# A late product with v and the next pair's transposes, each moved by one step in an attention and Fourier-mix kernel

## The chip, the cores and the metric

The kernel runs on one core of one Trainium2 chip. The metric is the device time of one execution in microseconds (us). All times in the text are in us unless a unit stands beside them.

## The reference

Attention with a threshold on 8 batches of 8 heads (576 rows of 64), and after it a Fourier mix and a two-layer network on rows of 512. Everything is float32.

```python
def _attn_ref(q, k, v, tau):
    scores = scale * np.matmul(q, k.transpose(0, 1, 3, 2))
    thresh = np.max(scores, axis=-1, keepdims=True) - tau
    scores = np.where(scores >= thresh, scores, -1000000000.0)
    scores = scores - np.max(scores, axis=-1, keepdims=True)
    attn = np.exp(scores)
    attn = attn / (np.sum(attn, axis=-1, keepdims=True) + 1e-09)
    return np.matmul(attn, v).astype(np.float32)
...
    X = np.fft.fft(x, axis=1)
    X = np.fft.fft(X, axis=2)
    u = x + np.real(X).astype(np.float32)
    un = (u - mu) / np.sqrt(var + 1e-06)
    ch = np.maximum(un @ w_ch1, 0.0) @ w_ch2
    return (u + ch).astype(np.float32)
```

Here x is the attention's output with the heads side by side, and mu and var are the mean and variance of each row of u.

## The kernel before, in words

**Pairs and steps.** The attention works on pairs of heads: four pairs a batch, 32 in all, numbered n from 0. A pair has five steps, t = 0 to 4. In the first four, 128 query rows of both heads are worked on; the fifth has the last 64 rows of both heads together. A step is written (n, t), and i = 5n + t. Every instruction of every engine stands in the order in which the program issues it (the schedule is made by hand), so what the loop issues first on an engine runs first there.

**The main loop** (L1774) runs over i from 40 on, that is from pair 8. In step i it issues, in this order:

1. `scores(i)`: q times k on TensorE into two score buffers (L439; in the fifth step L445, which reads a small copy of q made by `prep_ends`). The two buffers are those of the step before, so a score matmul waits until VectorE's last reading of them (L539).
2. For some steps the matmuls of a product with v (`values_in_parts`, L734). Each pair has two such products: part 0 for the query rows of t = 0 and 1, part 1 for those of t = 4, 2 and 3.
3. `softmax_first(i)`: two row maxima on VectorE (L518), then exponentials and a threshold on ScalarE (L524, L528).
4. The product's copies from PSUM to x on ScalarE (L740, L741 for part 1, L743 for part 0).
5. `fetch` for earlier steps (below), then `fill(True)`: a portion of the network's background work.
6. `softmax_second(i)`: compare, multiply and sum on VectorE (L539), and the reciprocal of the sum (L543, L546).
7. `decide(i - 1)`, `blocks(i - 1)`, some folding of x, `weights_in_parts(i - 1)`, `fill()`, `softmax_third(i)` (two ScalarE scalings, L552), `keep_blocks(i - 1)`, preparations for the next pair, and another `fill()`.

**Two ways for the weights.** The softmax's result e has to be turned round before it can be multiplied with v. Either TensorE transposes it and ScalarE copies it into the tile et_all (L637 to L668). Or, from pair 12 on and where `decide` says so, it goes through DRAM: VectorE transposes it in squares of 32 (`blocks`, L601) into one staging tile, ScalarE's queue writes that tile to DRAM as e_blocks (`keep_blocks`, L606), and the sync queue (SP) brings it back into et_all in four transfers (`fetch`, L615). There is one staging tile, so an L601 waits until the write before it has landed. `decide` picks the DRAM way for the first four steps of a pair when the background work is in the first of its two phases (`phase[0] == 1`), and for t = 2 after a DRAM step. In the trace these are (13,1) to (13,3), (14,0) to (14,3) and (15,0), and the same every four pairs up to (31,0): 40 steps.

**et_all** is in three groups of four blocks. t = 0 fills the first group, t = 1 and t = 2 the second in turn, t = 3 the third, t = 4 half of the first (blocks 2 and 3). Part 0 reads the first two groups; part 1 reads from block 2 on. So whatever writes blocks 2 and 3 for the next pair must come after part 1.

**When the products run, before.** Part 0 of pair n runs at the top of (n, 3), or at the top of (n+1, 0) if (n, 1) went through DRAM. Part 1 of pair n runs in (n+1, 1): at the top, or, if (n, 3) went through DRAM, after `fill(True)` with its copies right behind it (`late_values`, L1790 and L1805). There are ten such pairs: 13, 14, 17, 18, 21, 22, 25, 26, 29 and 30.

**The next pair.** q and k are loaded at the ends of (n, 0) and (n, 1), q is scaled on ScalarE in (n, 2), and `prep_pair(n + 1)` transposes them on VectorE at the end of (n, 3) (L410, L411, L413). `scores` of (n+1, 0) read the result. For pairs with their heads reversed (the first two of a batch) `v_of` makes a reversed copy of v on GpSimd (L584, L590); this happens in `weights_in_parts(i)` for t = 0, that is in step (n, 1).

**Background.** `fill` runs the network for groups of 512 rows as a budget allows: in phase 1 matmuls L1298 with additions on VectorE (L1235) and relus on ScalarE (L1240), in phase 2 matmuls L1447 with left-hand forms on VectorE and GpSimd (L1279). Their right-hand blocks are brought in through SP (L1171), in the same queue as the fetches, the loads of q, k and v, and the stores.

Of the kernel before, what the change touches and what calls it, by code (L numbers as in the profile page):

```python
# [47 lines left out]
def kernel(  # L48
# [13 lines left out]
    B, H, S, D = q.shape  # L62
# [3 lines left out]
    NPAIR = H // 2  # L66
    NT = 5
# [320 lines left out]
    heads = {}  # L388
# [171 lines left out]
    by_dma = {}  # L560
    phase = [0]

    def in_blocks(n):

        return n >= 3 * NPAIR
# [5 lines left out]
    def decide(i):  # L571

        n, t = divmod(i, NT)
        by_dma[i] = i < B * NPAIR * NT and in_blocks(n) and t < 4 and (
            phase[0] == 1 or t == 2 and by_dma[i - 1]
        )

    def v_of(n):

        src = heads[n][2]  # L580
        if PAIRS[n % NPAIR] % 2 == 0:
            return src
        vt = sb.tile([128, 10, D], FP32, tag="vr", bufs=1, name="v_rev")
        nc.gpsimd.tensor_copy(vt[:, :, 0:1], src[:, :, 0:1])  # L584
        last = src[:, :, D - 1 : D]
        down = bass.AP(
            tensor=last.tensor, offset=last.offset,
            ap=[list(last.ap[0]), list(last.ap[1]), [-1, D - 1]],
        )
        nc.gpsimd.tensor_copy(vt[:, :, 1:D], down)  # L590
        return vt
# [3 lines left out]
    def blocks(i):  # L595

        if not by_dma[i]:
            return
        e = steps.pop(i)[0]
        out_ = et_room.rearrange("p (b c q) -> p c b q", b=4, c=NC9)  # L600
        nc.vector.transpose(out_, e[:, 0 : 2 * S])  # L601
# [24 lines left out]
    def weights_in_parts(i):  # L626

        n, t = divmod(i, NT)
        if in_blocks(n) and t == 0:
            heads[n] = (*heads[n][0:2], v_of(n), None, None)  # L630
        if by_dma.get(i):
            return
        e, rec = steps.pop(i)
        if in_blocks(n) and t < 4:
            to = by_block[:, first_block(t) : first_block(t) + 4]
            pe = ps.tile([128, 4, 128], FP32, tag="mm", bufs=4, name="pe")
            nc.tensor.transpose(pe[:, 0, :], e[:, 512:640], ident[:, :])  # L637
            nc.scalar.copy(to[:, :, 4, :], pe[:, 0, :].rearrange("p (a q) -> p a q", q=32))  # L638
            for j in range(2):
                pw = ps.tile([128, 4, 128], FP32, tag="mm", bufs=4, name="pw")  # L640
                if j == 1:
                    yield
                for c in range(4):
                    c0 = (S + D) * j + 128 * c
                    nc.tensor.transpose(pw[:, c, :], e[:, c0 : c0 + 128], ident[:, :])  # L645
                nc.scalar.copy(
                    to[:, :, 5 * j : 5 * j + 4, :],
                    pw[:, :, :].rearrange("p c (a q) -> p a c q", q=32),
                )
            return  # L650
        if in_blocks(n):
            pe = ps.tile([128, 4, 128], FP32, tag="mm", bufs=4, name="pe")
            nc.tensor.transpose(pe[:, 0, :], e[:, 512:640], ident[:, :])
            for j in range(2):
                hp = slice(64 * j, 64 * j + 64)
                nc.scalar.copy(
                    by_block[hp, 2:4, 4, :],
                    pe[hp, 0, hp].rearrange("p (a q) -> p a q", q=32),
                )
            pw = ps.tile([128, 4, 128], FP32, tag="mm", bufs=4, name="pw")  # L660
            for c in range(4):
                nc.tensor.transpose(pw[:, c, :], e[:, 128 * c : 128 * c + 128], ident[:, :])
            for j in range(2):
                for a in range(2):
                    nc.scalar.copy(
                        by_block[:, 2 + a, 5 * j : 5 * j + 4, :],
                        pw[:, :, 64 * j + 32 * a : 64 * j + 32 * a + 32],
                    )  # L668
            return
        if t in (0, 2):  # L670

            e_t, ends = early_e_t, early_ends
            vt = v_of(n) if t == 0 else heads[n][2]
            heads[n] = (*heads[n][0:2], vt, e_t, ends)
        e_t, ends = heads[n][3:5]
        q0 = 128 * (t - (0 if t < 2 else 2))
        pe = ps.tile([128, 4, 128], FP32, tag="mm", bufs=4, name="pe")
        nc.tensor.transpose(pe[:, 0, :], e[:, 512:640], ident[:, :])  # L680
        kept = 1
        if rec is not None:
            nc.tensor.transpose(pe[:, 1, :], rec, ident[:, :])
            kept = 2
        if t < 4:
            nc.scalar.copy(ends[:, 0:kept, q0 : q0 + 128], pe[:, 0:kept, :])
        else:
            for j in range(2):
                hp = slice(64 * j, 64 * j + 64)
                nc.scalar.copy(ends[hp, 0:kept, q0 : q0 + 64], pe[hp, 0:kept, hp])  # L690
        qs = slice(q0, q0 + (128 if t < 4 else 64))
        for j in range(2 if t < 4 else 1):
            pw = ps.tile([128, 4, 128], FP32, tag="mm", bufs=4, name="pw")
            if j == 1:
                yield
            for c in range(4):
                c0 = (S + D) * j + 128 * c
                nc.tensor.transpose(pw[:, c, :], e[:, c0 : c0 + 128], ident[:, :])  # L698
            if t < 4:
                nc.scalar.copy(e_t[:, 4 * j : 4 * j + 4, qs], pw[:, :, :])  # L700
            else:
                nc.scalar.copy(
                    e_t[:, :, qs].rearrange("p (j c) q -> p j c q", j=2),
                    pw[:, :, :].rearrange("p c (j q) -> p j c q", j=2),
                )
# [846 lines left out]
    total = B * per_batch  # L1552
# [117 lines left out]
    def fold_more():  # L1670
        if folds and next(folds[0], True):
            folds.pop(0)
# [101 lines left out]
    for i in range(2 * per_batch, total + 3):  # L1774


        n, t = divmod(i, NT)
        values = iter(())
        if i < total:
            scores(i)  # L1780
        late_values = None
        if t == 3 and i < total and not by_dma.get(i - 2):
            values = values_in_parts(n, 0)
        elif t == 0 and by_dma.get(i - 4):
            values = values_in_parts(n - 1, 0)
        elif t == 1 and n > 0:
            while folds:
                fold_more()
            values = values_in_parts(n - 1, 1)
            if by_dma.get(i - 3):  # L1790
                values, late_values = iter(()), values
        next(values, None)
        if i < total:
            softmax_first(i)
        next(values, None)
        if t == 0 and by_dma.get(i - 4):
            fetch(i - 3)
        if t != 4 or not by_dma.get(i - 3):
            fetch(i - 2)
        if i % per_batch == 2:  # L1800
            for _ in last_fold:
                pass
            start_batch(i // per_batch - 1)
        fill(True)
        for _ in late_values or ():  # L1805
            pass
        if i < total:
            softmax_second(i)
        while held:
            held.pop(0)()  # L1810
        decide(i - 1)
        blocks(i - 1)
        while swaps:
            swaps.pop(0)()
        if mixes:
            mix(1)
        if t == 1:
            if n % NPAIR:
                folds.append(fold_rows(n - 1))
            else:  # L1820
                last_fold = fold_rows(n - 1)
                next(last_fold)
        weights = weights_in_parts(i - 1) if i <= total else iter(())
        next(weights, None)
        if t > 2:
            fold_more()
        fill()
        if i % per_batch == 1:
            next(last_fold)
        next(weights, None)  # L1830
        if i < total:
            softmax_third(i)
        keep_blocks(i - 1)
        if i < total:
            if t == 1:
                prep_ends(n)
            if t == 2 and n + 1 < B * NPAIR:
                scale_q(n + 1)
            if t == 3 and n + 1 < B * NPAIR:
                prep_pair(n + 1)  # L1840
        if wanted:
            wanted.pop().factors()
        if i % per_batch == 1:
            next(last_fold)
        fill()
        if t == 2 and n + 1 < B * NPAIR:
            load_v(n + 1)
        if t < 2 and n + 1 < B * NPAIR and len(loaded.get(n + 1, ())) == t:
            load_raw(n + 1, slice(t, t + 1))
# [50 lines left out]
```

## Time and profile before

| | |
|---|---|
| median of three runs | 1653.06 us (1650.37 to 1654.93) |
| the profiled execution | 1660.9 us |
| its span, first to last instruction | 1659.1 us |
| mean granted TensorE clock | 0.972 |
| transfers, mean over the span | 173 GB/s |

In the page's groups each line has the program's line, the engine, the operation with its output and inputs and their shapes, the count, the busy time and mean length, and after the bar the idle time of the engine just before these instructions with what ended most of it. In a timeline each line is a run of like instructions: start, length, engine, line, operation, and in square brackets the idle time ahead with its releaser. TensorE records two passes for each of these matmuls, so a count such as x20 stands for ten.

Steps differ in length with what they hold. In the stretch from pair 26 to pair 27 they run (start and length):

| step | start | length |
|---|---|---|
| (26,1) | 1138.4 | 9.4 |
| (26,2) | 1147.8 | 6.5 |
| (26,3) | 1154.3 | 6.3 |
| (26,4) | 1160.6 | 8.4 |
| (27,0) | 1169.0 | 11.0 |
| (27,1) | 1180.0 | 16.8 |
| (27,2) | 1196.8 | 7.3 |
| (27,3) | 1204.1 | 14.3 |

### The profile page before, as it was taken

The page shows a single profiled execution, that of the slowest core. Times are in us where ns is not written, and L with a number is a line of the kernel's source. Part 1 is how long each engine was busy: PE and PEld are TensorE (multiplying, and loading weights), DVE is VectorE, ACT ScalarE, POOL GpSimd, SP SyncE. Part 2 cuts the span into 40 slices and gives each one's busy share as a digit, 9 for nine tenths or more (in the row PEclk, how much of TensorE's full clock was granted, in tenths as well). Part 3 has the DMA queues.
Part 4 walks back from the last instruction along what each step waited for, and adds up shares of the span by engine and source line. Part 5 has one row for each costly group of instructions (what it writes and reads, how often), then busy time and mean ns, then how long its engine had stood idle before and what let it go on. Part 6 is the DMA issues. An engine that isn't in the chain of part 4 may idle for free.

```text
span 1659.1 us, 27069 instructions
## 1 busy us (share of the span) xinstructions
PE 1529.6 (92%) x9410; PEld 1166.8 (70%) x9410; DVE 1138.9 (69%) x2137; ACT 907.0 (55%) x1913; POOL 817.8 (49%) x1002
## 2 busy tenths in 40 slices
PE   8998889999999988999799988999799988999997
PEld 4555445556788766877588766787587767889987
DVE  7998786747678675767567765857567765645537
ACT  5765665545656565656466564666456655233231
POOL 6785663044454633544154724454154625546646
PEclk9999999999999998999999998999999999999999
DMA  6423222556855687648774777657775776657765
GB/s 160 120 55 111 73 73 50 191 174 169 256 168 143 177 225 208 186 110 230 199 201 135 196 220 208 175 131 219 208 195 129 213 210 189 205 152 218 245 183 194
DMA packets 296254, 286.26 MB, mean 173 GB/s; under 512 B 202643, under 2 KB 241045, under 8 KB 295222
## 3 DMA queue, kind: packets, MB, share of 16 engines
q1 hardware_dynamic: 287846, 260.64, 57.5%
q10 hardware_dynamic: 8272, 23.89, 4.0%
q8 instruction: 76, 1.25, 0.3%
q14 instruction: 60, 0.49, 0.1%
HBM read 231.10 MB, written 53.22 MB: 171 GB/s over the span
## 4 chain that ended last, share of the span: by engine, by line
PE 55%; DVE 19%; DMA 11%; ACT 7%; issue 4%; POOL 2%; SPq 1%; ACTq 0%; DVEq 0%; POOLq 0%
PE po L1447 14%; PE ph L1298 13%; PE pv L734 8%; PE sc L439 5%; PE po L1025 4%; DMA et_all<-e_blocks 3%; DMA w<-f 3%; DMA e_blocks<-w 2%; PE ph L1001 2%; ACT e L524 2%; DVE e L479 2%; PE pw L645 2%; DVE e L539 2%; PE pw L698 2%; PE py L874 2%
## 5 line engine op out<-in xcount | busy, mean ns | idle before, releaser
L524 ACT ACTIVATE e<-sc,neg 128x576 f32<-128x576 f32 x216 | 158.6, 734 | 132.3 <-DVE neg L518 131.5
L1447 PE MATMUL po<-w,w_all 128*128 128x128 f32 x1792 | 229.3, 278 | 1.2 <-ACT et_all L638 0.7
L518 DVE TENSOR_REDUCE neg<-sc 128x1 f32<-128x576 f32 x216 | 153.7, 748 | 110.0 <-PE sc L439 101.3
L1447 PEld LDWEIGHTS po<-w,w_all 128*128 128x128 f32 x1792 | 214.2, 193 | 11.5 <-issue 5.3
L1244 POOL TENSOR_TENSOR w<-hs 128x512 f32<-128x512 f32 x32 | 42.3, 1326 | 334.7 <-ACT hs L1240 334.7
L539 DVE SCALAR_TENSOR_TENSOR e<-sc,thr,e 128x576 f32<-128x576 f32 x216 | 168.3, 812 | 54.7 <-ACT thr L528 54.7
L1298 PE MATMUL ph<-u_t,w 128*128 128x256 f32 x768 | 183.0, 383 | 0.0
L439 PE MATMUL sc<-kT,qT 64*128 64x288 f32 x1024 | 171.2, 433 | 9.5 <-DVE e L479 9.0
L1298 PE MATMUL ph<-w_all,w 128*128 128x256 f32 x672 | 159.4, 384 | 12.0 <-DVE hs L1235 11.6
L552 ACT ACTIVATE e<-e,den 128x576 f32<-128x576 f32 x216 | 156.8, 769 | 24.2 <-DVE den L546 23.7
L1298 PEld LDWEIGHTS ph<-u_t,w 128*128 128x128 f32 x768 | 142.4, 190 | 29.8 <-issue 8.2
L1298 PEld LDWEIGHTS ph<-w_all,w 128*128 128x128 f32 x672 | 125.1, 190 | 42.8 <-issue 13.6
L734 PE MATMUL pv<-et_all,v_in 128*64 128x256 f32 (+1 forms) x640 | 106.5, 488 | 41.5 <-DMA et_all<-e_blocks 17.4
L1235 DVE TENSOR_TENSOR hs<-ph,hs 128x512 f32<-128x512 f32 x64 | 60.5, 945 | 119.5 <-PE ph L1298 114.3
L439 PEld LDWEIGHTS sc<-kT,qT 64*128 64x128 f32 x1024 | 94.1, 187 | 65.0 <-issue 36.3
L1347 POOL TENSOR_TENSOR w_all<-w_all 128x128 f32<-128x128 f32 (+2 forms) x160 | 121.8, 779 | 32.7 <-DVE w_all L1465 22.4
L1240 ACT ACTIVATE hs<-hs 128x512 f32<-128x512 f32 x64 | 54.0, 843 | 135.0 <-DVE hs L1235 135.0
L1447 PE MATMUL po<-w,hs 128*128 128x128 f32 x960 | 125.7, 278 | 0.0
L1447 PEld LDWEIGHTS po<-w,hs 128*128 128x128 f32 x960 | 116.6, 193 | 8.9 <-issue 7.5
L734 PEld LDWEIGHTS pv<-et_all,v_in 128*64 128x64 f32 x640 | 55.8, 163 | 88.5 <-issue 52.1
L734 PE MATMUL pv<-et_all,v_rev 128*64 128x256 f32 (+1 forms) x640 | 84.7, 411 | 7.3 <-DMA out_dram<-u 4.7
L916 POOL TENSOR_TENSOR u_t<-x,tmp 128x289 f32<-128x289 f32 (+1 forms) x45 | 34.7, 770 | 105.3 <-DVE tmp L911 105.3
(235 smaller groups left out, 3216.9 us busy)
## 6 DMA issues: line engine op xcount, KB each, us to landing
w<-f SPq DMA_DIRECT2D x304, 512.0 KB, 4.5
e_blocks<-w ACTq DMA_DIRECT2D x40, 576.0 KB, 3.7
et_all<-e_blocks SPq DMA_DIRECT2D x160, 144.0 KB, 4.3
hs<-in_moe_w_ch_dram SPq DMA_DIRECT2D x23, 512.0 KB, 4.6
q_in<-in_q_dram SPq DMA_DIRECT2D x128, 72.0 KB, 4.6
out_dram<-u SPq DMA_DIRECT2D x36, 256.0 KB, 4.3
k_in<-in_k_dram SPq DMA_DIRECT2D x124, 72.0 KB, 4.2
v_in<-in_v_dram SPq DMA_DIRECT2D x64, 128.0 KB, 4.7
```

Of the source, the lines that this page charges most:

```text
L439: nc.tensor.matmul(sc[j][:, c, 0:HALF], qT[hp, 128 * t : 128 * t + 128], kT[hp, k0 + HALF * c : k0 + HALF * (c + 1)], start=True, stop=True,)
L518: nc.vector.tensor_reduce(out=neg[:, j : j + 1], in_=sc[j][:, :, 0:HALF], axis=AXIS_XY, op=ALU.max, negate=True,)
L524: nc.scalar.activation(out=ej, in_=sc[j][:, :, 0:HALF], func=ACT.Exp, bias=neg[:, j : j + 1], scale=1.0)
L539: nc.vector.scalar_tensor_tensor(out=ej, in0=sc[j][:, :, 0:HALF], scalar=thr[:, j : j + 1], in1=ej, op0=ALU.is_ge, op1=ALU.mult, accum_out ...
L552: nc.scalar.activation(out=e[:, S * j : S * (j + 1)], in_=e[:, S * j : S * (j + 1)], func=ACT.Copy, scale=den[:, j : j + 1],)
L734: nc.tensor.matmul(pv[64 * j : 64 * j + 64, 0:m], vt[:, 2 * c + j, :], right, start=(c == 0), stop=(c == 4), skip_group_check=True,)
L1025: nc.tensor.matmul(po[:, :], hs[:, BT * j + 128 * t : BT * j + 128 * (t + 1)], w2[j], start=(j == 0), stop=(j == NJ - 1),)
L1235: nc.vector.tensor_tensor(out=to, in0=bank, in1=to if other is None else other, op=ALU.add)
L1240: nc.scalar.activation(out=to, in_=to, func=ACT.Relu)
L1298: nc.tensor.matmul(bank[:, 256 * q : 256 * q + 256].rearrange("p (two n) -> p two n", two=2), left[:, 256 * c + 128 * q : 256 * c + 128 * ...
L1347: return lambda: eng.tensor_tensor(out=to, in0=to, in1=other, op=ALU.add)
L1447: nc.tensor.matmul(to, lefts[m][j][:, s], right_[:, 128 * s : 128 * (s + 1)], start=fresh and s == 0, stop=s == 3, skip_group_check=True,)
```

## The change

Part 1 of a pair whose (n, 3) went through DRAM is issued one step later, at the top of (n+1, 2), with its copies where those of other products stand. For that, `decide` also sends a step t = 0 through DRAM when the step two before it went that way (`by_dma[i - 2]` is (n-1, 3)); v's reversed copy is made in (n, 2) after `fill(True)`, behind the product, and no longer in (n, 1); and the folding of that pair's x is put in the list in (n+1, 2). Apart from that, `prep_pair(n + 1)` is issued in (n, 4), right behind `blocks(i - 1)`, and no longer at the end of (n, 3). This second edit holds for all pairs of the main loop.

```diff
         by_dma[i] = i < B * NPAIR * NT and in_blocks(n) and t < 4 and (
-            phase[0] == 1 or t == 2 and by_dma[i - 1]
+            phase[0] == 1 or t == 2 and by_dma[i - 1] or t == 0 and by_dma[i - 2]
         )
...
     def weights_in_parts(i):
 
         n, t = divmod(i, NT)
-        if in_blocks(n) and t == 0:
-            heads[n] = (*heads[n][0:2], v_of(n), None, None)
         if by_dma.get(i):
             return
...
-        late_values = None
         if t == 3 and i < total and not by_dma.get(i - 2):
             values = values_in_parts(n, 0)
         elif t == 0 and by_dma.get(i - 4):
...
         elif t == 1 and n > 0:
             while folds:
                 fold_more()
+            if not by_dma.get(i - 3):
+                values = values_in_parts(n - 1, 1)
+        elif t == 2 and by_dma.get(i - 4):
             values = values_in_parts(n - 1, 1)
-            if by_dma.get(i - 3):
-                values, late_values = iter(()), values
         next(values, None)
...
         fill(True)
-        for _ in late_values or ():
-            pass
+        if t == 2 and i < total and in_blocks(n):
+            heads[n] = (*heads[n][0:2], v_of(n), None, None)
         if i < total:
             softmax_second(i)
...
         decide(i - 1)
         blocks(i - 1)
+        if t == 4 and n + 1 < B * NPAIR:
+            prep_pair(n + 1)
         while swaps:
             swaps.pop(0)()
         if mixes:
             mix(1)
-        if t == 1:
+        if t == (2 if by_dma.get(NT * n - 2) else 1):
             if n % NPAIR:
                 folds.append(fold_rows(n - 1))
             else:
+                assert t == 1
                 last_fold = fold_rows(n - 1)
                 next(last_fold)
...
                 prep_ends(n)
             if t == 2 and n + 1 < B * NPAIR:
                 scale_q(n + 1)
-            if t == 3 and n + 1 < B * NPAIR:
-                prep_pair(n + 1)
```

## The prediction

> **What bounds the kernel now.** I read the page first, then the waits of the tile pv, then TensorE's and VectorE's timelines of one cycle of four pairs, then the table by stretch. A step is named (pair, t). Its start is its first score matmul (L439, L445).
>
> ```profile
> PE 1529.6 (92%) x9410; PEld 1166.8 (70%) x9410; DVE 1138.9 (69%) x2137; ACT 907.0 (55%) x1913; POOL 817.8 (49%) x1002
> L734 PE MATMUL pv<-et_all,v_in 128*64 128x256 f32 (+1 forms) x640 | 106.5, 488 | 41.5 <-DMA et_all<-e_blocks 17.4
> ```
>
> TensorE is busy 92%, so a gain has to come from its idle time, or from time at a low clock. The products with v (L734) have 41.5 us of idle ahead of them, mostly put down to a transfer. TensorE from (26,4) to (27,3):
>
> ```profile
> 1161.77 1.89 PE L1298 MATMUL ph<-u_t,w 128*128 128x256 f32 x8
> 1165.35 1.99 PE L1298 MATMUL ph<-w_all,w 128*128 128x256 f32 x8 [1.70 <-DVE hs L1235]
> ...
> 1169.01 1.24 PE L439 MATMUL sc<-kT,qT 64*128 64x288 f32 x8
> 1171.56 2.38 PE L734 MATMUL pv<-et_all,v_in 128*64 128x256 f32 x20 [1.31 <-DMA et_all<-e_blocks]
> ...
> 1181.14 1.99 PE L1298 MATMUL ph<-w_all,w 128*128 128x256 f32 x8
> 1188.60 5.47 PE L734 MATMUL pv<-et_all,v_in 128*64 128x320 f32 x20 [5.47 <-DMA q_in<-in_q_dram]
> 1194.00 1.99 PE L1298 MATMUL ph<-w_all,w 128*128 128x256 f32 x8
> ...
> 1207.77 3.90 PE L734 MATMUL pv<-et_all,v_in 128*64 128x256 f32 x20 [2.46 <-ACT e L524]
> ```
>
> The columns are start, length, what ran, and in brackets the idle ahead. At 1188.60 stands the late second product of pair 26 in (27,1): 5.47 us idle, then 20 records in 5.47 us where 2.7 would do. A last transfer into et_all was issued at 1183.73; q_in, named as releaser, is not among its operands, so I take it as that landing. The first product of pair 27 waits too (1207.77). At 1165.35 TensorE waits for VectorE, whose timeline says why:
>
> ```profile
> 1161.64 1.36 DVE L601 STREAM_TRANSPOSE w<-e 128x1152 f32<-128x1152 f32 x1
> 1162.92 0.73 DVE L410 STREAM_TRANSPOSE kT<-k_in 128x576 f32<-128x576 f32 x1
> 1163.67 0.24 DVE L411 STREAM_TRANSPOSE kT<-k_in 64x64 f32<-64x64 f32 x1
> 1163.94 0.78 DVE L413 STREAM_TRANSPOSE qT<-q_in 128x576 f32<-128x576 f32 x1
> 1164.65 0.65 DVE L1235 TENSOR_TENSOR hs<-ph,hs 128x512 f32<-128x512 f32 x1
> ...
> 1168.64 1.38 DVE L601 STREAM_TRANSPOSE w<-e 128x1152 f32<-128x1152 f32 x1 [0.47 <-DMA e_blocks<-w]
> ```
>
> The add that TensorE wants (L1235) stands behind the next pair's transposes. The five late products of this kind by stretch (us, busy times, then clock, DMA share, GB/s), first and last:
>
> ```profile
> 1180.00:1196.80 16.80, 11.33 (x53) 7.01 (x52) 5.96 (x11) 3.45 (x8) 0.00 (x0) 0.80 0.70 156
> 1367.50:1382.20 14.70, 10.47 (x55) 6.77 (x54) 6.03 (x11) 3.52 (x8) 0.00 (x0) 0.88 0.54 138
> ```
>
> A step of 16.8 us with 6.0 us of VectorE and 3.5 of ScalarE in it, at 0.80 of the clock: idle, and half clock after it.
>
> **What the Trainium skill says.** "TensorE: Matmul & The Clock Gate", Part 1: after an idle window of about 3.4 us the clock is halved until a busy one has passed. The stretch 1188.5 to 1193.6 has a clock of 0.50, so it agrees; but 2.46 us of idle also brought 0.55 (1207.7 to 1211.2), and 1.31 us none. The same page, Architectural detail: VectorE and ScalarE take instructions strictly in order; the L1235 above shows it. "DMA: Bandwidth & Descriptors", Issuing engines are not separate DMA queues: transfers of all queues share the same 16 engines. In (26,4) the DMA share is 1.03 at 306 GB/s, and ScalarE's e_blocks write issued at 1163.03 ended its packets only 5.1 us later, against 2.4 in quiet steps.
>
> **The change part by part.** The steps through DRAM were read off the issues of e_blocks<-w: (13,1) to (13,3), (14,0) to (14,3), (15,0), and so on every four pairs, 40 in all. The new clause of `decide` (t = 0 after a DMA fourth step) adds none, since (14,0) and (15,0) are among them and (13,0) is not preceded by one. So ten late products move: five from (14,1) to (14,2) and five from (15,1) to (15,2), and their likes. Work per step, from the timeline's spacing: scores 1.17 us, eight L1298 records 1.72, eight L1447 0.88, a second product 2.7.
>
> *A, (15,1) and (15,2).* Starts of steps give 20.9, 23.3, 22.7, 24.2 and 21.9 us for the two, 113.0 in all. Without the product (15,1) holds 1.17 + 3.44 + 0.88 = 5.5 us of TensorE, and the score buffers come free when the second L539 ends, 5.4 us in: I take 5.7. (15,2) is 7.3 with no idle; with the product 10.0. From the end of pair 26's first product to the landing were 15.1 us (12.6 to 15.3 in the five); the new place comes after 6.5 + 5.7 + 1.2 = 13.4, so a wait of 0 to 1.9 stays, 0.8 on average: 16.5 a pair of steps, 82.5, a gain of 30.5. DMA share over these steps is 0.75 to 0.8; packed into two thirds of the time it comes near the 1.03 of (26,4), so I take 29 (18 to 34).
>
> *B, (14,1) and (14,2).* 15.6, 16.7, 15.8, 15.9, 15.7 = 79.7 now. After: 4.9 (6.4 in one) + 6.5 + 2.7; 72.0. Gain 7.7 (4 to 9).
>
> *C, first product in (15,3).* Idle and half clock cost 3.5, 3.8, 3.7, 4.0 and 0.8 us against the 10.3 that the fifth has without them. Its data waits in SP's queue for the write of e_blocks, which ScalarE issued late (1197.86), being held 9.5 us in front of the late product's copy (L740). That hold goes. But the fetch must now follow the product in (15,2), as both use blocks 2 and 3 of et_all. Landing and demand then fall together, some 11 us into (15,2). Gain 8 of 15.8 (0 to 14.6).
>
> *D, transposes at (13,4).* Three of them, 0.73 + 0.24 + 0.78 = 1.75 us, leave (13,3) and follow L601 of (13,4). (14,0)'s scores stand behind them, and everything on TensorE behind those. L601 needs the preceding e_blocks write landed, whose packets end 4.1 to 4.6 us in; I take 4.7, so it ends at 6.05, the transposes at 7.8, and the scores wanted to start at 6.83: 1.0 each, and 2.3 in (17,4), where the write is later. A loss of 6.3 (2 to 11).
>
> *E, at (14,4).* The 1.70 us wait for L1235 goes, so the next scores are due at 6.7. If the write lands as late as now, L601 ends at 9.4 and the transposes at 11.2; the first product of pair 14 starts 1.2 later, 1.4 to 2.0 after its present time, and the idle of 4.5 brings up to 1.7 of half clock: 13 in five, 21 if the shorter (14,1) only lengthens the queue of transfers. If the write lands in the 2.4 to 3.5 us of elsewhere, the product starts 0.5 to 1.9 earlier than now, when it waits for et_all: a gain of 5. I take a loss of 10.
>
> *F, the rest.* In the other 14 fifth steps VectorE ends its reciprocal 1.5 to 4.7 us ahead of the next scores, mostly over 2.6, which hides 1.75 us; in (19,4) 0.3 shows. L1279's forms move back by as much: loss 2 (0 to 6), and 25 if that cover were gone. `v_of` (0.2 + 0.7 us on POOL) moves a step later; L1279 waited 3.1 us for it, and the product that needs it comes a step later or more: nothing, and up to 1 us a pair if POOL were behind. On SP, pair 13's two swap transfers now stand in front of (14,0)'s fetch and wait for ScalarE's copy, as they did a step earlier: that fetch has two steps of room. `prep_pair` issues no transfer here; the next q load comes a step after its L413, and the v load that overwrites the late product's v stands at the end of the step that now holds the product, some 5 us after it: nothing. Folds still start from the fourth step on: nothing.
>
> Sum: 29 + 7.7 + 8 - 6.3 - 10 - 2 = 26.4 us. The profiled execution took 1660.9 us (span 1659.1), 7.8 above the median 1653.1 of the runs; it would come to 1634.5, the median to 1627.
>
> **Rivals.** *Slower: the transposes take the place of the wait.* In ten fifth steps scores stand behind L601 and 1.75 us, and each idle passes the clock gate: 4.0 + 1.7 = 5.7 each, 57 us, with C nothing and A and B 38: 1653 + 19 = 1672. It decides from about 4 us for each of the ten. For it: L601 at 1168.64 already waits for a landing. Against: in (13,4) it does not. *No change: transfers bind.* A gives 18, B 4, C 2, the losses stay at 18: 1647. For it: share 1.03 in (14,4). Against: 0.54 to 0.8 where the long idle is. *More: every landing comes earlier*, as ScalarE and SP are not held: A 32, B 9, C 14, D -2, E 0, F 0: 1600. For it: the 9.5 us hold. That nothing moves is excluded: ten products change place.
>
> **Chances.** Forecast 0.69 (1610 to 1642), transfers bind 0.10, transposes 0.09, more 0.12. A measurement of this kernel can tell some 0.3%, 5 us, from none. Faster: 0.67 + 0.12 + 0.05 = 0.84; same 0.02 + 0.04 = 0.06; slower 0.10. Range 1604 to 1648: it leaves out the transposes' rival and the best of "more".
>
> **What would show it.** A right: L734 has no idle in (15,1), (15,2) some 10 us, clock 1.0 in both. C: idle ahead of L734 in (15,3) under 1 us. D and E: L439 waits for L413, some 1 us in (14,0), 2 to 4.5 in (15,0), and no 1.70 <-DVE hs L1235. Wrong: over 10 us of L439 idle beyond that, or an L734 that still waits over 2 us at t = 2.

## The result, and the profile after

The changed kernel takes 1681.1 us (median of four runs, 1680.5 to 1682.9) where the kernel before, on the same chip, took 1654.0 (1650.4 to 1656.2): a ratio of 1.0168, 95% interval 1.0147 to 1.0189. It is **27 us slower**; 26 us less were forecast. One execution of kernel 5 below fell into a slow state (3045 us) and is left out of its numbers. The profiled execution took 1680.6 (span 1678.8, clock 0.963), 19.7 more than that of before.

From line 630 on, the changed kernel's lines are two lower than those of the kernel before (L734 is now L732, L1298 is L1296, L1235 is L1233). The lines of its page that answer to those of the prediction, and the scores beside them:

```profile
PE 1522.4 (91%) x9410; PEld 1164.0 (69%) x9410; DVE 1132.8 (67%) x2137; ACT 907.0 (54%) x1913; POOL 818.4 (49%) x1002
L439 PE MATMUL sc<-kT,qT 64*128 64x288 f32 x1024 | 174.5, 444 | 40.6 <-DVE qT L413 30.5
L732 PE MATMUL pv<-et_all,v_in 128*64 128x256 f32 (+1 forms) x640 | 94.5, 445 | 41.1 <-DMA et_all<-e_blocks 39.2
```

TensorE does the same work in a little less busy time (mean product record 445 ns after 488), so the loss is idle time on it. The products' own idle is as long as before (41.1 and 41.5), though the late products no longer wait; and the scores, which had 9.5 us of idle, have 40.6, put down to the q transpose L413. So two waits are new. TensorE's timeline in (27,0) and (27,2) shows where (start, length, idle ahead in brackets):

```profile
1184.76 2.29 PE L439 MATMUL sc<-kT,qT 64*128 64x288 f32 x8 [4.43 <-DVE qT L413]
1194.56 4.54 PE L732 MATMUL pv<-et_all,v_in 128*64 128x256 f32 x20 [7.51 <-DMA et_all<-e_blocks]
...
1213.15 2.91 PE L732 MATMUL pv<-et_all,v_in 128*64 128x320 f32 x20
```

At 1213.15 stands the moved product of pair 26, in (27,2): no idle ahead, 2.91 us. That is what the change was made for. But (27,0), from 1184.76, begins with 4.43 us of idle for the transposes and goes on with 7.51 for the data of the pair's *first* product, and both the scores (2.29 for 1.24) and the product (4.54 for 2.38) then run at half clock (0.50 in both stretches). VectorE's timeline shows the first of the two:

```profile
1181.60 1.38 DVE L601 STREAM_TRANSPOSE w<-e 128x1152 f32<-128x1152 f32 x1 [3.13 <-DMA e_blocks<-w]
...
1183.92 0.78 DVE L413 STREAM_TRANSPOSE qT<-q_in 128x576 f32<-128x576 f32 x1
```

L601 waits for a landing, and the three transposes (the last is shown) queue behind it. The second wait needs SP's queue. Here a length holds the waits between the transfers of one group; first the kernel before with the fetches of (26,0) and (26,1), then the changed one with the load of the next q and the same two fetches:

```profile
1152.66 7.23 SPq L615 DMA_DIRECT2D et_all<-e_blocks  x4
...
1163.13 3.69 SPq L615 DMA_DIRECT2D et_all<-e_blocks  x4
```

```profile
1153.85 9.78 SPq L140 DMA_DIRECT2D q_in<-in_q_dram  x4
...
1171.41 1.74 SPq L615 DMA_DIRECT2D et_all<-e_blocks  x4
...
1178.79 13.08 SPq L615 DMA_DIRECT2D et_all<-e_blocks  x4
```

The fetch of (26,1), which the first product of pair 26 reads, took 3.7 us to issue and takes 13.1. Its first transfer goes out at 1178.79, its second only at 1190.60. The changed kernel's waits say for what (us in total, times, longest):

```profile
SPq L615 <- DMA e_blocks<-w: 69.6, 13, 11.7
SPq L140 <- DMA e_blocks<-w: 57.2, 9, 9.5
```

The longest wait of a fetch for an e_blocks write is 11.7 us (5.6 before). It isn't its own write: that of (26,1) was issued at 1168.51. Loads of q and k (L140), which read no e_blocks at all, wait for such writes too; in the kernel before none does. The write that landed just before 1190.60 is ScalarE's write of (26,3), issued at 1187.81:

```profile
1185.90 1.06 ACT L1238 ACTIVATE hs<-hs 128x1024 f32<-128x1024 f32 x1 [8.21 <-DVE hs L1233]
...
1187.81 0.33 ACTq L606 DMA_DIRECT2D e_blocks<-w  x1
```

What has the fetch of one step to do with the write of a later one? The built program tells. All 1076 transfers of SP and ScalarE take one of eight semaphores in turn, in one common order, and before each issue its queue waits until the transfer eight places earlier has landed. The places around (26,4), from the two programs:

```
before   801 ACT write of (26,3)   804-807 SP fetch of (26,1)   809 SP load of a weight block (f2)
after    797 ACT write of (26,3)   804-807 SP fetch of (26,1)   805 = its second transfer
```

Before, eight places behind the write is a weight load that comes after the fetch. Now it is the fetch's second transfer. So SP stands still from 1179.4 until that write has landed at 1190.6, and ScalarE issues it behind a relu (L1238) that waits for VectorE's add (L1233), which stands behind the transposes. I call this a hold: a queue stands still for a transfer whose data it doesn't need.

By step, sums of the five cycles (starts of steps):

| steps | before | after | difference | forecast |
|---|---|---|---|---|
| (15,1), (15,2) | 113.0 | 84.5 | -28.5 | A -29 |
| (14,1), (14,2) | 79.7 | 72.7 | -7.0 | B -7.7 |
| (15,3) | 67.3 | 55.7 | -11.6 | C -8 |
| (13,4), (14,0) | 85.2 | 94.1 | +8.9 | D +6.3 |
| (14,4), (15,0) | 102.5 | 159.5 | +57.0 | E +10 |

Four of the five lines are near their forecast; the last (20.0 of it in (14,4), 37.0 in (15,0)) is off by 47 us.

### The profile page after: what moved, and what is told of

Read it like the earlier page. It is cut to its first block, busy times and chain, and to the rows that moved or that the text cites. A ratio compares the mean times of both kernels' runs of the same rounds, so it can differ in the third digit from the quotient of the medians.

```text
span 1678.8 us, 27060 instructions
## 1 busy us (share of the span) xinstructions
PE 1522.4 (91%) x9410; PEld 1164.0 (69%) x9410; DVE 1132.8 (67%) x2137; ACT 907.0 (54%) x1913; POOL 818.4 (49%) x1002
## 4 chain that ended last, share of the span: by engine, by line
PE 56%; DVE 19%; DMA 8%; ACT 6%; issue 5%; POOL 3%; SPq 2%; ACTq 0%; DVEq 0%; POOLq 0%
PE po L1445 15%; PE ph L1296 13%; PE pv L732 8%; PE sc L439 6%; PE po L1023 3%; DMA e_blocks<-w 3%; DMA et_all<-e_blocks 2%; PE ph L999 2%; DVE e L539 2%; PE pw L643 2%; DVE e L479 2%; PE py L872 2%; PE pw L696 1%; DVE hs L1233 1%; ACT e L524 1%
## 5 line engine op out<-in xcount | busy, mean ns | idle before, releaser
L439 PE MATMUL sc<-kT,qT 64*128 64x288 f32 x1024 | 174.5, 444 | 40.6 <-DVE qT L413 30.5
L1296 PE MATMUL ph<-u_t,w 128*128 128x256 f32 x768 | 183.8, 384 | 1.0 <-ACT hs L1309 1.0
L1296 PEld LDWEIGHTS ph<-u_t,w 128*128 128x128 f32 x768 | 143.0, 191 | 32.1 <-issue 8.2
L1296 PE MATMUL ph<-w_all,w 128*128 128x256 f32 x672 | 158.5, 383 | 6.0 <-DVE hs L1233 6.0
L439 PEld LDWEIGHTS sc<-kT,qT 64*128 64x128 f32 x1024 | 95.9, 192 | 96.8 <-issue 36.9
L1296 PEld LDWEIGHTS ph<-w_all,w 128*128 128x128 f32 x672 | 125.6, 190 | 32.0 <-DVE hs L1233 9.8
L1238 ACT ACTIVATE hs<-hs 128x512 f32<-128x512 f32 x64 | 54.0, 843 | 161.2 <-DVE hs L1233 161.2
L732 PE MATMUL pv<-et_all,v_in 128*64 128x256 f32 (+1 forms) x640 | 94.5, 445 | 41.1 <-DMA et_all<-e_blocks 39.2
L1233 DVE TENSOR_TENSOR hs<-ph,hs 128x512 f32<-128x512 f32 x64 | 60.1, 939 | 87.7 <-PE ph L1296 82.5
L732 PEld LDWEIGHTS pv<-et_all,v_in 128*64 128x64 f32 x640 | 49.1, 149 | 84.6 <-issue 55.2
L800 POOL TENSOR_TENSOR half<-x 128x287 f32<-128x287 f32 x48 | 41.3, 881 | 103.0 <-DMA x<-swap 87.2
L1277 DVE TENSOR_TENSOR w_all<-hs 128x512 f32<-128x512 f32 x40 | 47.9, 1198 | 62.0 <-ACT hs L1313 53.3
```

What stands on the lines that cost most here:

```text
L439: nc.tensor.matmul(sc[j][:, c, 0:HALF], qT[hp, 128 * t : 128 * t + 128], kT[hp, k0 + HALF * c : k0 + HALF * (c + 1)], start=True, stop=True,)
L732: nc.tensor.matmul(pv[64 * j : 64 * j + 64, 0:m], vt[:, 2 * c + j, :], right, start=(c == 0), stop=(c == 4), skip_group_check=True,)
L1233: nc.vector.tensor_tensor(out=to, in0=bank, in1=to if other is None else other, op=ALU.add)
L1238: nc.scalar.activation(out=to, in_=to, func=ACT.Relu)
L1296: nc.tensor.matmul(bank[:, 256 * q : 256 * q + 256].rearrange("p (two n) -> p two n", two=2), left[:, 256 * c + 128 * q : 256 * c + 128 * ...
```

## The experiments

**Theory.** Two waits in series make the loss. The transposes of the fifth step stand behind L601, which waits for a landing; and the fetch of (14,1) stands eight places behind the write of (14,3), so it waits for that write. **Rivals.** The transposes alone (they delay everything, the fetch too); the order or the traffic of the transfers alone. Ratios are to the kernel before, measured beside each kernel on the same chip; its median was 1654.8 to 1656.9. Kernels 1 to 4, 5 to 8, 9 to 11 and 12 were measured apart, so across these groups the ratios compare better than the medians.

| kernel | edit | median us | ratio, 95% interval |
|---|---|---|---|
| 1 | late products moved only | 1666.8 | 1.0066 (1.0041 to 1.0091) |
| 2 | transposes moved only | 1668.9 | 1.0087 (1.0057 to 1.0117) |
| 3 | changed kernel, v loaded in the fifth step | 1665.0 | 1.0049 (1.0033 to 1.0066) |
| 4 | kernel 1, v loaded in the fifth step | 1647.5 | 0.9942 (0.9918 to 0.9966) |
| 5 | kernel 4, four tiny transfers ahead of the fetch | 1664.1 | 1.0052 (1.0033 to 1.0072) |
| 6 | kernel 4, the same four behind it | 1652.4 | 0.9985 (0.9970 to 1.0001) |
| 7 | changed kernel, writes from GpSimd's queue | 1718.2 | 1.0363 (1.0327 to 1.0399) |
| 8 | kernel 1, writes from GpSimd's queue | 1691.9 | 1.0208 (1.0183 to 1.0232) |
| 9 | kernel 4, q and k loaded together | 1667.1 | 1.0070 (1.0045 to 1.0096) |
| 10 | kernel 4, k loaded a step later in (15,2) | 1636.0 | 0.9880 (0.9845 to 0.9916) |
| 11 | the edits of 9 and 10 | 1653.2 | 0.9981 (0.9966 to 0.9996) |
| 12 | kernel 10, transposes in the fifth step ahead of L601 | 1639.1 | 0.9909 (0.9886 to 0.9931) |

### 1 and 2: each part of the change alone

Kernel 1 is the changed kernel with `prep_pair` put back:

```diff
-        if t == 4 and n + 1 < B * NPAIR:
-            prep_pair(n + 1)
...
+            if t == 3 and n + 1 < B * NPAIR:
+                prep_pair(n + 1)
```

Kernel 2 is the kernel before with only that edit the other way round.

> The late products move, the transposes stay at the end of the fourth step. Theory (two waits in series: the next scores stand behind the moved transposes, some 4.5 us in each (14,4); and the second transfer of the fetch of (14,1) holds SP's queue until the e_blocks write of (14,3) has landed, because the two are eight places apart in the order of all transfers, and the transposes also delay that write): the L439 waits of the pair's fifth step go, the write comes 1.8 us earlier, the wait of the first product in (15,0) falls from 7.5 to some 5.5 us but stays: some 1630 us. Rival, transposes alone: both waits go, some 1600 us. Rival, order of transfers alone: the wait in (15,0) stays at 7.5 us and the time within 15 us of the changed kernel's 1681: 1666 to 1681.

> The transposes move to the fifth step, the late products stay. Here the transfer eight places after the write of (14,3) is a weight load that comes after the fetch of (14,1), as in the kernel before. Theory (two waits): L439 waits some 1 to 2 us in (14,0) and 4 to 5 in (15,0) with half clock after it, no long wait of the first product in (15,0): 1653 + 5 x (1.5 + 4.5 + 1) = some 1685 us, less what the later wait of the late product in (15,1) takes up, so 1665 to 1690. Rival, transposes alone: the same or more, with the wait of the first product in (15,0) at 7 us too: 1700. Rival, order of transfers alone: within 8 us of the kernel before.

Kernel 1 was expected at 1630 and took 1666.8: the theory had the right wait but thought it smaller. The time alone would also fit the order of the transfers as the only cause (1666 to 1681). TensorE in its (27,0), and SP's fetch of (26,1):

```profile
1170.14 1.24 PE L439 MATMUL sc<-kT,qT 64*128 64x288 f32 x8
1181.67 4.42 PE L732 MATMUL pv<-et_all,v_in 128*64 128x256 f32 x20 [10.28 <-DMA et_all<-e_blocks]
```

```profile
1167.76 11.21 SPq L615 DMA_DIRECT2D et_all<-e_blocks  x4
```

The scores no longer wait, and the product waits 10.28 instead of 7.51: the landing is the later of the two, so what the scores gain the product loses. Over the five cycles (14,4) and (15,0) take 49.8 and 102.5, 50 us more than before the change, without one transpose moved. The product alone, meant to gain 45, loses.

In kernel 2 the write is again eight places ahead of a weight load. L439 waits 3.4 to 4.0 us in (15,0) and 1.5 to 2.9 in (14,0), the first product of the pair 1.2 to 2.5, and (15,1), where the late product still stands, is 18.9 shorter, since its data have had more time: 1668.9, inside the expected 1665 to 1690. Each part alone costs, so neither rival in its pure form holds: the transposes alone don't explain kernel 1, and the order of transfers alone allowed kernel 2 no more than 8 us above the kernel before, where it is 12.

### 3 and 4: another transfer eight places behind the write

```diff
-        if t == 2 and n + 1 < B * NPAIR:
+        if t == 4 and n + 1 < B * NPAIR:
             load_v(n + 1)
```

> The changed kernel with the next pair's four v transfers issued at the end of the fifth step instead of the third. The transfer eight places after the write of (14,3) is then a weight load behind the fetch of (14,1), no longer the fetch itself. Theory (two waits): the fetch of (14,1) is issued a step earlier, the wait of the first product in (15,0) falls from 7.5 us to under 2.5, the L439 waits stay: 1681 - 5 x (5 + 2 of half clock) = some 1645 us. Rival, transposes alone: the fetch still follows the late write for another reason, L732 still waits over 5 us, 1670 to 1685. Rival, order of transfers alone: L439's waits shrink as well, 1620.

> The late products move, the transposes stay in the fourth step, and the v transfers are issued in the fifth: neither of the two waits. Theory (two waits): no L439 wait over 1.5 us in (14,0) or (15,0), no wait of the first product in (15,0) over 2.5 us; A, B and C of the prediction stay: 1653 - 45 = some 1605 us. Rival, transposes alone: the same as with the late products alone (first run of this group), within 5 us. Rival, order of transfers alone: the same as the changed kernel with the v transfers in the fifth step (third run of this group), within 5 us. If transfers bind: 1640 or more.

SP in kernel 4:

```profile
1155.60 3.52 SPq L615 DMA_DIRECT2D et_all<-e_blocks  x4
1159.22 9.71 SPq L1169 DMA_DIRECT2D w<-f  x3
```

The fetch issues in 3.5 us; the hold is now in the weight loads behind it (9.71), where TensorE doesn't wait for it. (15,0) falls from 102.5 to 66.4 (kernel 1 to 4) and from 97.5 to 61.0 (changed kernel to 3), and the time by 19 and 16 us. Kernel 3's first product in (15,0) waits in one cycle of five (2.4 us), as the theory has it, but the kernel missed the expected 1645 by 20 us: (15,3) takes 68.7 where the changed kernel took 55.7, and (13,4) with (14,0) 5.8 more. Kernels 3 and 4 also price the transposes without the hold: 17.5 us between their medians, where the prediction had 18.3 for D, E and F. That the two agree is in part luck: by steps D's differ by 13.4 us (6.3 said), E's by 6.7 (10 said).

Kernel 4 is faster than the kernel before, but by 9 us and not by the 48 expected: its first product in (15,0) still waits 1.2 to 3.9 us, (14,4) is 8.7 longer and (15,3) 1.8. Some 5 of the 8.7 are in (18,4) and are a hold again: the load of a weight block stands eight places behind the write of (18,2), SP waits for that write from 787.5 to 791.6, and TensorE then waits 3.58 us for the block. For the rest the rival of transfers that bind is open (1640 or more was its sign): while kernel 4 fetches (26,1), from 1155.6 to 1165.6, the DMA share is 0.96.

### 5 and 6: the place alone

Moving the v loads also takes four transfers and their bytes out of the fetch's way. So kernel 4 got four transfers of 4 bytes, in kernel 5 at the end of the third step (t == 2), where the v loads were, in kernel 6 at the end of the fifth (t == 4):

```diff
+        for j in range(4):
+            nc.sync.dma_start(out=tiny[:, j : j + 1], in_=v[0, 0, 0:1, j : j + 1])
...
+        if t == 2 and n + 1 < B * NPAIR:
+            load_tiny()
         if t == 4 and n + 1 < B * NPAIR:
             load_v(n + 1)
```

> The fourth kernel (late products moved, transposes in the fourth step, v loaded in the fifth) with four transfers of 4 bytes where the v loads stood, at the end of the third step. They carry nothing, but the write of (14,3) is then eight places ahead of the second transfer of the fetch of (14,1) again. Theory (shared semaphores): that transfer is held until the write has landed, the first product in (15,0) waits 8 to 10.5 us again where the fourth kernel waited 1.2 to 3.9, and the time is near the late products alone: 1647 + 5 x 4 = some 1665 us. Rival (it is the traffic of the v loads, or their length in SP's queue, that made the fetch late): within 6 us of the run after this one, about 1650.

> The same four transfers of 4 bytes, but at the end of the fifth step, behind the fetch of (14,1); the eighth place after the write of (14,3) is a weight load as in the fourth kernel. Both theories: 1647 to 1652 us, the first product in (15,0) waits under 4 us. If the transfers of 4 bytes cost something by themselves, this run shows it.

Here the fetch is L622 and the product L739. Kernel 5, then kernel 6, SP and TensorE:

```profile
1165.96 3.43 SPq L157 DMA_DIRECT2D tiny<-in_v_dram  x4
1169.43 9.70 SPq L622 DMA_DIRECT2D et_all<-e_blocks  x4
```

```profile
1181.90 4.34 PE L739 MATMUL pv<-et_all,v_in 128*64 128x256 f32 x20 [9.48 <-DMA et_all<-e_blocks]
```

```profile
1172.36 4.76 SPq L622 DMA_DIRECT2D et_all<-e_blocks  x4
...
1185.48 1.17 SPq L157 DMA_DIRECT2D tiny<-in_v_dram  x4
```

```profile
1176.94 3.23 PE L1303 MATMUL ph<-t_room,w 128*128 128x256 f32 x8 [3.13 <-DMA w<-f]
...
1181.88 2.38 PE L739 MATMUL pv<-et_all,v_in 128*64 128x256 f32 x20 [0.18 <-ACT e L564]
```

Sixteen bytes a pair, put ahead of the fetch, bring its hold back (9.70 us) and the product's wait with it (9.48); (15,0) takes 99.3 against 66.1. The two kernels have the same transfers and the same computation, and 1664.1 and 1652.4 us, with intervals that do not touch. That decides for the place, against traffic and length of the queue. The hold costs less in all than in its step: of the 33 us between the two in (15,0), (15,3) gives back 23 (56.7 in kernel 5, 80.0 in kernel 6).

In kernel 6 the product in (19,0) still waits 7.3 us, over the 4 expected. That is a hold too. Eight places behind the write of (18,2), issued at 795.14, now stands the transfer that brings a swapped row back (L772 here), which is ahead of the fetch of (18,1) in SP's queue:

```profile
SPq L772 <- DMA e_blocks<-w: 6.7, 1, 6.7
```

This one wait ends at 801.5, when the write lands.

### 7 and 8: the write in a queue of its own

```diff
-            nc.scalar.dma_start(out=scratch[i % 3][:, :], in_=et_room)
+            nc.gpsimd.dma_start(out=scratch[i % 3][:, :], in_=et_room)
```

> The changed kernel with the e_blocks writes issued from GpSimd's queue in place of ScalarE's; nothing of SP's transfers then waits for a write except the fetch of that write. Theory: SP's stalls at the q loads and at the fetch of (14,1) go, the first product in (15,0) waits under 2.5 us, L439's waits for the transposes stay: some 1645 us, if GpSimd takes up the write within 1 us of L601; up to 1690 where the write stands behind GpSimd's own work, which would show as L601 waiting longer for e_blocks<-w. Rival (transposes alone): the first product in (15,0) still waits over 5 us and the time is within 8 us of the changed kernel's 1681.

> Late products moved, transposes in the fourth step, e_blocks writes from GpSimd's queue. Theory: neither of the two waits, so the prediction's A, B and C without D to F: 1653 - 45 = 1608 us at best, 1625 if C does not come; more where GpSimd is late with the writes. Rival (transfers bind whatever the order): no faster than the fourth kernel's 1647.

The wait of the first product in (15,0) goes in both, as the theory has it (all idle ahead of the group L732 that reads v_in is 8.6 and 9.5 us). In kernel 7 that proves less, as the scores ahead of the product come 6.6 to 9.5 us late and give its data time; in kernel 8 they don't wait. But both are slower: 7 is 28 us over the 1690 that was allowed for a late GpSimd, 8 is far above its 1608 to 1625. GpSimd, too, takes up the write only behind its earlier work. Kernel 7's page and its GpSimd queue:

```profile
L601 DVE STREAM_TRANSPOSE w<-e 128x1152 f32<-128x1152 f32 x40 | 54.7, 1368 | 85.9 <-DMA e_blocks<-w 85.9
```

```profile
1213.63 1.47 POOL L832 TENSOR_TENSOR f<-f 128x608 f32<-128x608 f32 x1
1215.04 0.58 POOL L606 DMA_DIRECT2D e_blocks<-w  x1
```

The write of an L601 that ended at 1213.08 stands behind the folds of x, the next L601 waits for its landing 6.2 us, and the scores 8.5. One hold was exchanged for another.

### 9 to 12: can it be made faster than both?

```diff
# 9
+        if t == 0 and n + 1 < B * NPAIR and not loaded.get(n + 1, ()):
+            load_raw(n + 1, slice(0, 2))
...
# 10: k at t == 2 where n % 4 == 3 and in_blocks(n)
-        if t < 2 and n + 1 < B * NPAIR and len(loaded.get(n + 1, ())) == t:
+        if t in (0, 2 if in_blocks(n) and n % 4 == 3 else 1) and ...
# 12: kernel 10, and
+        if t == 4 and n + 1 < B * NPAIR:
+            prep_pair(n + 1)
         decide(i - 1)
         blocks(i - 1)
```

> The fourth kernel (1647.5 us) with the next pair's q and k both loaded at the end of the first step instead of q there and k a step later. In the fourth kernel the transfer eight places after the write of (14,1) is the first of the fetch of (14,0), in this one a swap. Theory (shared semaphores): the fetches of (14,0) and (14,1) come some 2 us earlier, the first product in (15,0) waits under 2 us (1.2 to 3.9 in the fourth), 5 x 2 = 10 us less: some 1638 us. Rival (the transfers themselves bind there, the DMA share being near 1): within 5 us of the fourth kernel.

> The fourth kernel with the next pair's k loaded a step later in (15,2), so that the fetch of (15,0) stands ahead of k in SP's queue. Theory: that fetch goes out about 1.5 us earlier, right after the landing of its write, the idle ahead of the first product in (15,3) falls from 1.9 to 4.9 us to under 1.5 with less half clock after it: 5 x 2 = some 1637 us. Rival (the write's own landing binds, not k's place): (15,3) as before and 1645 to 1650 us.

> The two edits of the runs before this one together. Theory: both gains, some 1628 us, the prediction's forecast without its D to F being 1608. Rival (transfers bind): 1645 or more.

> The tenth kernel (1636 us) with the transposes in the fifth step as in the changed kernel, but ahead of the block transpose L601 of that step instead of behind it. Theory (what costs in the fifth step is that the transposes stand behind L601, which waits for the landing of the e_blocks write before, not their 1.75 us): L439 waits some 1 to 2.5 us in (15,0) instead of 4 to 5.6, the 1.5 us in (14,4) go, and the time is within 8 us of the tenth kernel: 1630 to 1644. Rival (any place in the fifth step costs what it cost between the third and the fourth kernel, 17 us): 1650 to 1656 us.

**9** missed by 29 us. I had followed two writes and not the third: eight places behind the write of (14,2) (788) now stands the first transfer that brings a swapped row back (796), and it is ahead of the fetch of (14,1) in SP's queue. SP in kernel 9:

```profile
1163.29 0.43 SPq L1169 DMA_DIRECT2D w<-f  x1
1169.57 1.14 SPq L765 DMA_DIRECT2D x<-swap  x2
...
1171.37 1.85 SPq L615 DMA_DIRECT2D et_all<-e_blocks  x4
```

SP stands still from 1163.8 to 1169.6; that write was issued at 1164.41 and landed at 1169.55. It is the same mechanism through another door, as in kernel 6's (19,0), found after the run and not tried by itself. **11** inherits it: 1653.2 where 1628 was expected.

**10** came out as expected in time, 1636.0, but by luck: the idle ahead of the product in (15,3) is 2.3 to 2.6 us in four cycles, not under 1.5, and its profiled execution (1640.6) is as long as that of kernel 4 (1641.3). That 10 beats the kernel before is measured; whether and why it beats 4 stays open (the ratios' intervals, from two measurements, all but touch: 0.9916 and 0.9918).

**12** puts the transposes into VectorE's wait for the landing instead of behind it:

```profile
1154.96 0.78 DVE L410 STREAM_TRANSPOSE kT<-k_in 128x576 f32<-128x576 f32 x1
...
1156.02 0.78 DVE L413 STREAM_TRANSPOSE qT<-q_in 128x576 f32<-128x576 f32 x1
1158.54 1.38 DVE L601 STREAM_TRANSPOSE w<-e 128x1152 f32<-128x1152 f32 x1 [1.73 <-DMA e_blocks<-w]
```

The scores of (15,0) don't wait for them at all, and the time, expected at 1630 to 1644, is 1639.1: 3 us over kernel 10 by the medians and 5 by the ratios, whose intervals overlap. So the fifth step is no bad place for them; behind L601 is.

## Why the prediction was wrong, point by point

**A** was right: 28.5 us for 29. In the changed kernel no L732 stands in (15,1), which is 6.8 each time (5.7 said), (15,2) takes 10.1 without the 0.8 of wait that was said, and the clock of (15,1) is 1.00. The DMA share there is 0.47 to 0.96, so the feared congestion came without a wait.

**B** was right: 7.0 for 7.7.

**C** was near in the changed kernel, 11.6 for 8, with 0 to 1.6 us of idle left, but by luck. It isn't a gain of the move as such: in kernels 3, 4 and 6, which have the move but not the long wait in (15,0), (15,3) takes 69, 69 and 80 us and nothing is gained. I suppose that the long wait lets the transfers catch up; that was not tried, and kernel 12 (57.7 without a long wait) and kernel 9 (71.7 with one) don't fit it.

**D** was right in kind and a little small: L439 waits 1.3 to 2.4 us in (14,0) and 3.75 in (18,0), 8.9 us for 6.3.

**E** is where the loss stands: 57 us (20 in (14,4), 37 in (15,0)) for 10, with 21 as its worst case. Its first half held. It had L601 end at 9.4, and the transposes at 11.2, and L439 waits 4.35 to 5.1 us in four of the five cycles, where 4.5 was said. What failed is the sentence "the first product of pair 14 starts 1.2 later". It takes the fetch of (14,1) as landed by then. In four cycles the product waits another 7.5 to 7.9 us for it, in (19,0) 4.2, and half clock follows: the five steps (15,0) have clocks of 0.63 to 0.82, where three of the five had 1.00 before. In the cycle without a wait of the scores, (18,4), TensorE waits 4.85 us for the weight block that is held as in kernel 4. Kernel 1 shows that the product's wait does not need the transposes (50 of the 57 us come without them), kernels 5 and 6 that the place among eight semaphores makes it.

**F** holds the step that failed: what the change does to SP's queue was put at nothing, and kernel 1 shows that it is worth 50 us in E's steps. F says of the fetch of (14,0) "that fetch has two steps of room". For that fetch alone this is so; what was not asked is what stands behind it, and which transfers wait for which. In the kernel before it began 4.9 us into (26,2), at 1152.66, now it begins 14.3 us into it, at 1171.41. It does not wait for the moved product, which reads the blocks that it overwrites: that ended at 1161.2. Ahead of it the third transfer of the next q is held 7.7 us, until 1162.76, for the write of (26,0), eight places in front, and the fetch's own first transfer 2.7 us for the write of (26,1). The fetch of (14,1) stands behind all that and lost its slack. Kernel 4 has these holds too (its loads of q and k wait 59.0 us for writes in ten waits) and keeps 1.2 to 3.9 us of wait in (15,0); that they make this wait was not tried by itself. On top comes the hold of the fetch of (14,1). I had not thought of holds: I followed each wait of SP to data, and these waits have no data behind them. It could have been read off the waits of the kernel before:

```profile
SPq L1171 <- DMA e_blocks<-w: 43.1, 5, 9.4
```

These are weight loads, which have nothing to do with e_blocks, waiting 43.1 us for its writes in five waits: one hold a cycle, which then cost nothing.

**The sum.** Between the 1627 that was said and 1681 lie 54 us. The hold makes 16 to 19 of them (from the changed kernel to 3, from kernel 1 to 4). The transposes make none, as they cost in all what was said. The other 35 are missing in kernel 4 already: A, B and C were to bring 44.7 us there and bring 9. By steps A and B are there (26 and 7 us), C is not, and (14,4) and (15,0) are 14 us longer. About 10 us can't be placed, since the profiled execution is 8 us above the median in the kernel before and 6 below it in kernel 4.

The rival "transposes take the place of the wait" came nearest in sign and size (1672), and was about half of the 34 us between the changed kernel and kernel 4. It put 5.7 us on each of ten fifth steps and C at nothing; measured were D's 8.9, E's 57 and C's 11.6, so that its 57 in all is E's 57 only by chance. "Transfers bind" is not what made the changed kernel slow: in kernels 5 and 6 the same transfers give two times. For what kernel 4 lacks it is open. The two signs that I had named for a wrong prediction both stayed out: L439's idle in (14,0) and (15,0) is 28.8 us, where 27.5 was said at most and the sign needed over 10 more, and no product waits at t = 2. I had named no sign for the first product in (15,0), where the loss then was.

The half clock had its part again. "TensorE: Matmul & The Clock Gate", Part 1, in the Trainium skill puts the fall at an idle window of about 3.4 us; here 4.43 us of idle halved the clock (1.24 to 2.29 for the scores), which agrees, but in kernel 6 an idle of 3.13 ahead of L1303 already made its eight records take 3.23 where 1.97 is usual, with a clock of 0.50 in their second half. So in this kernel less than 3.4 us was enough.

## What to carry to other kernels

When a transfer is moved, or anything that changes the order of transfers, follow each queue past data: if the program shares a few completion semaphores among all transfers in turn, a queue can be held by an unrelated transfer of another engine, so list the transfer that stands that number of places behind every slow one and see what is queued behind it. A hold that costs nothing where it stands is a warning all the same: any change of the order can put it ahead of a transfer that is wanted, as kernels 1, 6 and 9 show. Work that is to fill a gap on an engine that takes its instructions in order belongs ahead of the instruction that waits, not behind it: the transposes cost 17 us behind L601 (kernels 3 and 4) and nothing clear of noise ahead of it (kernels 10 and 12).

## What the runs showed that was not expected

- Four transfers of 4 bytes moved the time by 12 us with their place alone (1664.1 and 1652.4). By themselves they cost SP 1.17 us of issue for the four, but even behind the fetch they change which transfers are eight places apart: kernel 6 is 5 us over kernel 4.
- A wait that two causes make at once is paid once, for the most part: taking the transposes away from the changed kernel took some 4.4 us of L439's idle out of (27,0) and put 2.8 onto the product's.
- GpSimd issued an e_blocks write in 0.58 us, ScalarE in 0.33, with landings of 3.5 us at the median on both; what made GpSimd's queue the worse one was what stood ahead of the writes in it.
